# An mLSTM, mixture-of-experts and ELU network on one core: recurrent state by float16 products and DMA copies, with a new order of the pieces

## The chip, the core and the metric

The kernel runs on one core of one Trainium2 chip. The core has TensorE (matrix products, results in PSUM), VectorE, ScalarE, GpSimd (POOL in the profile) and SyncE (SP), which here only starts transfers, and 16 DMA engines. The metric is the device time of one execution in microseconds (us).

## The reference

```
attention, per (b, h) and token t, D = 40, 2 x 8 heads, 768 tokens:
  m' = max(f + m, i); fs = exp(f + m - m'); is = exp(i - m')
  C = fs C + is v k^T;  n = fs n + is k
  y = sigmoid(o) * (C q) / max(|n q|, 1)
x = rows of y, 1536 x 320
experts: logits + log1p(exp(x w_noise)) * noise, best two of 8 per row, softmax weights
  x = sum over both of weight * (relu(x w1[e]) w2[e]),  w1 320 x 1024, w2 1024 x 320
last layer: out = ELU(x w_in) w_out,  w_in 320 x 2048, w_out 2048 x 320
```

Inputs and output are float32 (the last layer's weights reach the kernel as float64 words, from which it makes float32 itself).

## The kernel before, in words

The 1536 tokens are 12 chunks of 128, six for each batch, and chunks 0 to 5 are also the first half of the rows, 6 to 11 the second. The first piece of work is the gates (lines 498 to 528): the gates come in as 16 rows of 768, a scan on VectorE makes the running maximum, TensorE turns them into columns (`gate_cols`, L508), and two products with constant masks (L521, L522) and exponentials give the decays of every chunk.

Then, for each chunk (`attention`), k and q are split into float16 parts of 40 rows each, three parts to a head, turned on TensorE (L704, L705) and multiplied (L707); the product is masked (L709 or L710 with L712). The state of a batch (`st`, 40 x 8 x 41, float32) is carried from chunk to chunk: TensorE adds the new outer products (L676) to the old state, which a float32 product with the unit matrix puts into the same PSUM sum (L681), and VectorE multiplies by the decay (L684). For the heads of the next chunk the state has to be in 120 rows: high part, low part and high part again. That is made by a float32 product with a threefold unit matrix (`rep`, L686), a copy on ScalarE that rounds it to float16 (L690), and a VectorE piece that takes the high part away in the middle 40 rows (L691). The heads (L742, L745) then give the chunk's output, which is divided, multiplied by the sigmoid and handed to `token_rows`.

`token_rows` finds the greatest value of each row (L631 or L632), makes a power of two of it and its inverse (L634, L636), splits the row into float16 parts (`split_row`), stores it in DRAM (`x_rows`), turns it on TensorE (`turn_row`, L589) and multiplies it with the router's weights (L646); L649 scales the logits. After the last chunk of a half, `router` picks two experts for each row and makes the lists of rows for each expert.

There are 16 jobs, expert by half (`expert`). A job gathers its rows by indirect DMA (L977), has them turned by DMA (L585, on SP's queue), multiplies them with the expert's first weights (`contract`, L941, in four pairs of hidden blocks) and with its second weights (L954, L955, L957). All float32 weights are split into two float16 parts on ScalarE and VectorE when they arrive (L386, L397). After all jobs the rows are gathered again, mixed, and go through the last layer.

None of this is issued in the order of the code. Each call of `do` (class `Order`) records a piece with its inputs, outputs and the engines that may run it. `run` decodes the table `ORDER`: each number is four times the index of a piece, in the order in which the code records them, plus the choice of its engine. So the table fixes for every engine in which order it issues its work, DMA starts included, and an engine that waits for one piece holds up all that stands behind it:

```
order = np.frombuffer(zlib.decompress(base64.b85decode("".join(table.split()))), "<u2").tolist()
order = [divmod(x, 4) for x in order]
for i, j in order:
    ...
    op["ways"][j][2]()
```

Of the kernel before, what the change touches and what calls it, by code (L numbers as in the profile page):

```python
# [71 lines left out]
c-jTQZRC1;f&lREIp=$xpP!$;=hUTL4J{2VT^f4P($LVZhL(n2bm`L4i)J-6G_?HwH1wjSOG`sbLzk9bbZN+HX=!O_XlPbLFS;}|v~+3M&j$bq3LuWvF$N  # L72
TY02E*V2OtmyF^~WatO81)3J?|tH4w$#SO&DP6i9<4Xkrl01AsR{8yjFbFvU99uQ3K6VqGxD1iS^hSOb*70$XAuJdTgBf5RLsgV%wAPw^f$!FynX8~6~PU
|BqgId~R~@eizzbwD4iu)o1eL<URZDSVCX@EktF5kAMS_yDv)9-n|Mo5s^vj!>{IzQ;G%7BjE|Ucd`Po><^TT)=i%6fY8E5W`FOxA+||<G;gC_yaE!P2!1
Ph&^^DD#Q{`U={p~zwn<DJ)%uq@Hf7~KM_}=ir4U;69=qHtnnKGh$Gg5kmwU#;)D%|Hv9lz;x&SSbI^q&Fa%RjCq#(gkYI=gJ|aGYcjA9Bfl!DJykHF?iz
zS$Ki~pfu^je<W8#-^LNxIMJ0%SGARHKn29d|^*o=4*|BS!k1|;ABj$sE+LYL^l8F;}yxdd(eS8xjo7$T++kVEp%*o$}*b0SLo2hqcy7$S!-1tFP+Gx*oU
8Y~F_A)LbuWXLm{AU@$)7$-*Xg{_Fs$RiNQ4>AW2AW5dk8@48X2=`z>Zix-CfJ>Mn`uGa2;RbGDj9P&%{yDKHVq^gh@Hlw|OEOJn$OM@se@lEr{x=+vMYx
9wxg#^g0VatOJi;CEKV*_B!wSriHTWgW5@&dV7m%Qi#ECeNSC}Uo&>(MY3`=2a@&=pm4jnQ|Jz$+_Fmb9tRjDtiBDNv_o;s3aaz{0p7Sm=rOqb~~A55PaF
hgd<jF}U823xW~PM9-Ur~ZjrQ!DC1PMHarqKf2<nUX7}M3$&Eb0wS9g}s9fwPCi@jGU7@b_cdhn!1rYrcCXbEA^tv<O5V;h00LhQdz1*KS7Qv(s$|&{!Ep
ypO80tLEgz0bzrV+g)Y-aW>4j*Cv~9ORF&*dUFt6spikgI_oyRPBLQ}&?<}M{^obhK5Ay%WGWH94&sOO(^`seEpnLQU{40H8F3g2`kqZ4mzv&uXCqF2RG3  # L80
YY`8J2ml3e%^rOq2X2)gT>uL<>xvzA+W-O(MEMx5+X6WKHG;0Cj-_YR)W}C_SW_G^8Nbq8Z9zj%*bZI0pMUiI@@9BHQ$fKCuQjp{MkW?vg!nPAk-3(J!`!
#pwmTq@zrX5h%cosW+=|CN-hrjKfW-E;pkROoDc(C6lC+%!*DiX*xysxh$P#zNXeRqBiv3(OY^)@3;lEr1Erv%P?6c#}sJD?ddy{XOi53KGA=md)$aCFhy
p-Js5^NaAl^#q__*+<F9m@t1>l4V2|_%H{=x7U>z2*Q8vcL*#w(p5f|lBY>eA;B__>g*eo08p3IobaBn8ZzL-2a<+5CcE^tL|!WGyWTW1?=iK}o6uF00UB
# [1332 lines left out]
```

## Time and profile before

| | |
|---|---|
| time, median of three runs | 468.0 us (467.3 to 468.56) |
| the profiled execution | 472.35 us, span 470.6 us |
| TensorE busy | 440.8 us, 94% of the span |
| VectorE busy | 380.8 us, 81% |
| ScalarE busy | 300.8 us, 64% |
| GpSimd busy | 94.4 us, 20% |
| mean granted clock of TensorE | 0.984 |

The span runs from the first to the last instruction. A matmul's record is longer than the distance to the next one, since matmuls overlap; where work stands back to back, the pieces of the chain of waits show the pace. Float32 products have two records each.

### The profile page before, as it was taken

How to read it: one execution, taken by the hardware profiler on the slowest of the kernel's cores; microseconds unless marked ns; L12 is line 12 of the kernel's file. 1: busy time of each engine (PE TensorE's matmuls, PEld its weight loads, DVE VectorE, ACT ScalarE, POOL GpSimd, SP SyncE). 2: the span in 40 equal slices, each digit the busy share in tenths (PEclk: the TensorE clock that was granted, in tenths of full speed). 3: DMA queues.
4: the chain of work that ended last, by engine and by line, in shares of the span. 5: the costliest groups of instructions: out<-in, count | busy, mean ns of one | idle time of the engine just before them, and what ended most of it. 6: DMA issues, size and time to landing. Idle time of an engine off the chain costs nothing.

```text
span 470.6 us, 10573 instructions
## 1 busy us (share of the span) xinstructions
PE 440.8 (94%) x4094; PEld 372.1 (79%) x4094; DVE 380.8 (81%) x853; ACT 300.8 (64%) x519; POOL 94.4 (20%) x110
## 2 busy tenths in 40 slices
PE   4999889788899999999989999899999999999994
PEld 4788877677788979888868888788888877887873
DVE  5889999988998987998787897498788949678780
ACT  4798998675766764565564345398785765667640
POOL 3223125513121012112203102521321120000000
PEclk9999999879999999999989999999999999999999
DMA  9979574799996799799787942433302320001001
GB/s 132 175 138 183 143 138 102 204 238 245 241 302 185 217 239 299 188 198 262 207 231 223 262 142 63 114 91 33 72 21 79 84 43 30 1 27 31 1 31 33
DMA packets 102554, 66.43 MB, mean 141 GB/s; under 512 B 79216, under 2 KB 94112, under 8 KB 102496
## 3 DMA queue, kind: packets, MB, share of 16 engines
q1 hardware_dynamic: 99616, 57.27, 51.3%
q0 software_dynamic: 2816, 8.31, 6.8%
q8 instruction: 34, 0.56, 0.5%
q14 instruction: 24, 0.20, 0.1%
q10 hardware_dynamic: 64, 0.10, 0.1%
HBM read 50.87 MB, written 8.52 MB: 126 GB/s over the span
## 4 chain that ended last, share of the span: by engine, by line
PE 65%; DMA 14%; DVE 11%; ACT 4%; issue 3%; SPq 1%; POOL 1%; ACTq 0%; DVEq 0%
PE S L941 28%; PE O L954 10%; PE O L955 10%; PE O L957 9%; DMA sw<-in_moe_w 5%; DMA sf<-in_moe_w_in 3%; DVE wa L397 2%; PE O L742 2%; PE S L676 1%; DVE wb L397 1%; DMA xT<-xg 1%; DMA kt<-in_k 1%; PE T L704 1%; DMA x_rows<-xr 1%; DVE xr L397 1%
## 5 line engine op out<-in xcount | busy, mean ns | idle before, releaser
L941 PE MATMUL S<-xT,wa 128*128 128x224 f16 (+1 forms) x1024 | 102.0, 259 | 5.2 <-DMA xT<-xg 3.0
L941 PEld LDWEIGHTS <-wa 128*128 128x128 f16 x1024 | 95.2, 100 | 9.0 <-DMA xT<-xg 2.6
L941 PE MATMUL S<-x3T,fwa 128*128 128x256 f16 x768 | 88.7, 273 | 1.2 <-DMA x3T<-x3r 1.2
L941 PEld LDWEIGHTS <-fwa 128*128 128x128 f16 x768 | 75.1, 98 | 11.7 <-issue 1.5
L954 PE MATMUL O<-wb,hidden 128*128 128x320 f16 (+1 forms) x256 | 75.6, 300 | 2.1 <-ACT yo L377 0.9
L955 PE MATMUL O<-wb,hidden 128*128 128x320 f16 (+1 forms) x256 | 75.5, 300 | 0.0
L957 PE MATMUL O<-wb,hidden 128*128 128x320 f16 (+1 forms) x200 | 60.0, 300 | 0.7 <-DVE hidden L998 0.7
L977 POOL DMA_INDIRECT xg<-x_rows,table x32 | 36.0, 1126 | 114.7 <-DMA xT<-xg 94.0
L954 PE MATMUL O<-fwb,gh 128*128 128x320 f16 x192 | 57.4, 299 | 0.0
L955 PE MATMUL O<-fwb,gh 128*128 128x320 f16 x192 | 57.4, 299 | 0.0
L996 ACT ACTIVATE hidden<-S 128x448 f16<-128x448 f32 (+1 forms) x64 | 32.4, 512 | 25.3 <-PE S L941 25.0
L1159 DVE SCALAR_TENSOR_TENSOR ex<-ex,th 128x512 f32<-128x512 f32 x48 | 33.4, 697 | 14.1 <-ACT ex L1157 7.2
L998 DVE SCALAR_TENSOR_TENSOR hidden<-S,hidden 128x128 f16<-128x128 f32 (+2 forms) x92 | 39.8, 455 | 4.9 <-ACT hidden L996 4.6
L1158 ACT ACTIVATE re<-S,sca 128x512 f32<-128x512 f32 x48 | 32.9, 691 | 13.4 <-DVE gl__5588 L397 4.5
L1156 ACT ACTIVATE th<-S,sca 128x512 f32<-128x512 f32 x48 | 33.0, 686 | 13.1 <-PE S L941 13.0
L1157 ACT ACTIVATE ex<-S,sca 128x512 f32<-128x512 f32 x48 | 32.8, 686 | 10.3 <-PE S L941 9.5
L1119 POOL DMA_INDIRECT yg<-y_rows,rows_i x24 | 25.0, 1043 | 66.2 <-DVE fwb L397 27.9
L1160 DVE SCALAR_TENSOR_TENSOR re<-ex,re 128x512 f32<-128x512 f32 x48 | 32.9, 689 | 3.7 <-ACT re L1158 1.7
L1075 ACT ACTIVATE nm<-sf 128x320 f32<-128x320 f32 (+1 forms) x28 | 16.1, 576 | 28.5 <-DVE fwb L397 8.8
L955 PEld LDWEIGHTS <-hidden 128*128 128x128 f16 (+1 forms) x256 | 26.9, 105 | 8.9 <-issue 2.0
L954 PEld LDWEIGHTS <-hidden 128*128 128x128 f16 (+1 forms) x256 | 26.9, 105 | 7.9 <-ACT hidden L996 0.9
L397 DVE SCALAR_TENSOR_TENSOR wa<-sw,wa 128x1024 f16<-128x1024 f32 x24 | 28.9, 1217 | 4.0 <-ACT wa L386 3.8
(251 smaller groups left out, 864.5 us busy)
## 6 DMA issues: line engine op xcount, KB each, us to landing
sw<-in_moe_w SPq DMA_DIRECT2D x16, 512.0 KB, 4.3
sw<-in_moe_w SPq DMA_DIRECT2D x16, 480.0 KB, 4.3
sf<-in_moe_w_out SPq DMA_DIRECT2D x16, 320.0 KB, 3.7
sw<-in_moe_w SPq DMA_DIRECT2D x16, 256.0 KB, 5.1
sf<-in_moe_w_in SPq DMA_DIRECT2D x8, 512.0 KB, 5.8
sw<-in_moe_w SPq DMA_DIRECT2D x8, 320.0 KB, 4.5
y_rows<-yo SPq DMA_DIRECT2D x16, 160.0 KB, 4.4
sf<-in_moe_w_in SPq DMA_DIRECT2D x8, 256.0 KB, 4.9
```

The lines of the kernel that those rows point to most:

```text
L397: some(on, [("V", 0.07 + 0.06 * m + 1.04e-3 * n, lambda: V.scalar_tensor_tensor(dst(), src(), scale(), hi(), op0=OP.mult, op1=OP.subtract) ...
L941: PE.matmul(acc, wa[:, r, w, f * P:(f + 1) * P], xT[:, j, :n], start=(i == 0), stop=(i == 7))
L954: PE.matmul(o, a, wb[:, 0, f % FB], start=(f == 0), stop=False)
L955: PE.matmul(o, a, wb[:, 1, f % FB], start=False, stop=(not b and f == last))
L957: PE.matmul(o, b[0], wb[:, 0, f % FB], start=False, stop=(f == last))
L977: do([("G", 1.1, lambda: G.indirect_dma_start(out=xg()[:n], out_offset=None, in_=(x_all if hf else x_rows[0]())[:, :], in_offset=bass.Indi ...
L998: vec(2 * n, lambda x=x, n0=n0, n=n: V.scalar_tensor_tensor(hi(x, n), src(n0, n), 0.0, hi(n0, n), op0=OP.max, op1=OP.subtract), [ph, hid[f ...
L1156: act(512, lambda: A.activation(th(), pf(), AF.Tanh, scale=sca()[:, 2:3]), [pf, sca], [th], "exp", 1)
L1157: act(512, lambda: A.activation(ex(), pf(), AF.Exp, scale=sca()[:, 1:2]), [pf, sca], [ex], "exp", 1)
L1158: act(512, lambda: A.activation(re(), pf(), AF.Relu, scale=sca()[:, 1:2]), [pf, sca], [re], m=1)
L1159: vec(512, lambda: V.scalar_tensor_tensor(ex(), ex(), 1.0, th(), op0=OP.add, op1=OP.mult), [ex, th], [ex], port=True)
L1160: vec(512, lambda: V.scalar_tensor_tensor(re(), ex(), 0.0, re(), op0=OP.min, op1=OP.add), [ex, re], [re], port=True)
```

## The change

What it does, part by part:

- **Constant products.** Eight pieces of three products of 384 columns each, of constants, into columns of a PSUM bank that nothing reads.
- **State.** L681 becomes two float16 products with the unit matrix, of the state's high part and its low part. L686, L690 and L691 go. Instead a high part (40 rows, ScalarE or VectorE) and a low part (VectorE) are made from the state in SBUF, and two DMA copies per step bring the high part to rows 80 to 119 and the low part to rows 40 to 79 (20 copies in all). The high and low parts have three buffers.
- **First jobs.** The rows of jobs (0, 0), (1, 0) and (2, 0), six tiles, are turned by five transposes each on TensorE and one copy from PSUM, instead of by DMA.
- **Row scales.** The power of two of a row is made for six chunks at once, and the logits of a half are scaled in one piece; per chunk one small VectorE piece is left and a plain copy of the logits on VectorE or ScalarE. The scratch of the row maximum on ScalarE is the row buffer itself.
- **Constants.** `rep` and `less` and the clearing of the state go.
- **Order.** A new table, of 2025 pieces against 2009. Decoded, it has one piece of constant products ahead of the gate turns, one before L521, one after L522 and five between pieces of the attention (chunks 2 to 11). All 20 copies stand on SP. Nine of the ten high parts are on ScalarE, and nine of the twelve logit copies. The first expert products stand behind the logits of chunk 11, where they stood behind those of chunk 9. Ahead of the second half's L813 stand three pairs of hidden blocks (four before) and seven VectorE splits of expert weights (nine before). In SP's order the second weight load of expert 0 stands behind the row store of chunk 5 and the third behind the loads of k, q and v of chunk 11; before, both stood among loads of chunks 6 to 8. Further on the order differs in many places.

The diff, with the lines of the table left out:

```
--- before.py
+++ after.py
@@ -42,13 +42,15 @@
 NBLK = 256
 
 WIDE = 120
+FILL = 8
+EARLY = ((0, 0), (1, 0), (2, 0))
 
 SQ, SK, SV = 16.0, 4.0, 64.0
 SO = SQ * SK * SV
 SW = 128.0
 SIN, SOUT = 64.0, 128.0
 
-ON = dict(k3="A", q3="AV", vw="V", s3h="GA", s3l="V", ph="A", pl="GV", vh="VA", vl="V", y="G", xr="AVG", turn="AV",
+ON = dict(k3="A", q3="AV", vw="V", s3h="AV", s3l="V", ph="A", pl="GV", vh="VA", vl="V", y="G", xr="AVG", turn="AV",
           kq="AV", yo="VA", wh="AV", hv="VA", wl="V", q3l="V")
 PREC = "112111111111"
 
@@ -69,42 +71,42 @@
 
 
 ORDER = """
...
 """
 
 PASSES = ((0, 0, 0), (0, 1, 0), (1, 0, 1), (1, 1, 1), (3, 0, 0), (4, 0, 1), (2, 0, 2), (2, 1, 2))
@@ -507,6 +509,9 @@
         for c in range(NCH):
             PE.transpose(quarters(p())[:, j, c * BH:(c + 1) * BH], x()[:, o + c * P:o + (c + 1) * P], id32()[:BH, :BH])
 
+    for _ in range(FILL):
+        te(3, 384, lambda: [PE.matmul(bank[:, :384], ones16(), ones16()[:, None].to_broadcast([P, 3, P]),
+                                      start=True, stop=True) for _ in range(3)])
     vec(1, lambda: V.memset(mt()[:, 0:1], -1e30), [], [mt])
     vec(2 * S, lambda: V.tensor_tensor_scan(mt()[:, 1:], gf(), gi(), -1e30, op0=OP.add, op1=OP.max), [gf, gi], [mt])
     te(12, P, lambda: [gate_cols(p1, gf, 0, 0), gate_cols(p1, gi, 0, 1)], [gf, gi], [p1], rows=BH, busy=BH)
@@ -569,7 +574,7 @@
         pool(128, lambda: G.affine_select(out=before(), in_=before(), pattern=[[1, P]], compare_op=OP.is_gt,
                                           fill=0.0, base=0, channel_multiplier=-1), [before], [before])
 
-    inv2 = fixed([P, NT], F32, "inv2")
+    inv2, top = fixed([P, NT], F32, "inv2"), fixed([P, NT], F32, "top")
     logits = fixed([P, NT, 2 * E], F32, "logits")
 
     def split_row(xr, x, scale, r):
@@ -587,21 +592,12 @@
             return
         pt = ps_t()
         te(5, P, lambda: [PE.transpose(pt()[:, x, :n], xr()[:n, x * P:(x + 1) * P], id16()[:n, :n])
-                          for x in range(5)], r, [pt], w)
+                          for x in range(5)], r, [pt], [x[0] if isinstance(x, tuple) else x for x in w])
         copy(5 * n, lambda: dst()[:, :, n0:n0 + n], lambda: pt()[:, :5, :n], [pt], w, 0.52e-3, ON["turn"])
 
 
     st = [fixed([P, H, D1], F32, f"st{b}") for b in range(B)]
-    rep = fixed([P, 3, D], F32, "rep")
-    V.tensor_copy(rep(), id32()[:, :D].unsqueeze(1).to_broadcast([P, 3, D]))
-    for x in st:
-        V.memset(x(), 0.0)
-    less = fixed([P, 1], F32, "less")
-    G.memset(less(), -1.0)
-    for lo_row, step in ((-D, 1), (2 * D - 1, -1)):
-        G.affine_select(out=less(), in_=less(), pattern=[[0, 1]], compare_op=OP.is_ge, fill=0.0, base=lo_row,
-                        channel_multiplier=step)
-    s3 = {}
+    s3, slo = {}, {}
     U = {}
 
     def chunk(x, t):
@@ -625,17 +621,13 @@
 
         b, c = divmod(t, NCH)
 
-        am, sc = a_([P, 1], F32, "am"), a_([P, 1], I32, "sc")
-
-        far = a_([P, DM + 1], F32, "far", 1)
+        sc, xr = a_([P, 1], I32, "sc"), a_([P, ROW], F16, "xr", 3)
+        am = lambda: top()[:, t:t + 1]
         do([("V", 0.07 + 1.04e-3 * DM, lambda: V.tensor_reduce(am(), y(), axis=AX.X, op=OP.max, apply_absolute_value=True)),
-            ("A", 0.22 + 0.83e-3 * DM, lambda: A.activation(far(), y(), AF.Abs, scale=1.0 / 64, accum_out=am()))],
-           [y], [am])
-        chain([(1, lambda: V.tensor_scalar(inv2()[:, t:t + 1].bitcast(I32), am().bitcast(I32), EXPM, None,
-                                           op0=OP.bitwise_and)),
-               (1, lambda: V.tensor_scalar(sc(), inv2()[:, t:t + 1].bitcast(I32), EXPM, None, op0=OP.bitwise_xor))],
-              [am], [inv2[t], sc])
-        xr = a_([P, ROW], F16, "xr", 3)
+            ("A", 0.22 + 0.83e-3 * DM, lambda: A.activation(xr()[:, :DM + 1], y(), AF.Abs, scale=1.0 / 64, accum_out=am()))],
+           [y], [top[t], xr])
+        vec(1, lambda: V.tensor_scalar(sc(), am().bitcast(I32), EXPM, EXPM, op0=OP.bitwise_and, op1=OP.bitwise_xor),
+            [top[t]], [sc])
         split_row(xr, lambda: y()[:, :DM], lambda: sc().bitcast(F32), [y, sc])
         load(lambda: [(x_rows[b]()[c * P:(c + 1) * P], xr())], [x_rows[b]], [xr])
         xT, lg = a_([P, 5, P], F16, "xTt"), ps_l()
@@ -646,8 +638,7 @@
                 PE.matmul(lg()[:, :2 * E], xT()[:, j], (rwl if w else rwh)()[:, r], start=(n == 0), stop=(n == 7))
 
         te(8, 2 * E, logit, [xT, rwh, rwl], [lg])
-        vec(80, lambda: V.tensor_scalar(logits()[:, t], lg()[:, :2 * E], inv2()[:, t:t + 1], 0.5 / SW,
-                                        op0=OP.mult, op1=OP.mult), [lg, inv2[t]], [logits[b]])
+        copy(2 * E, lambda: logits()[:, t], lambda: lg()[:, :2 * E], [lg], [logits[b]])
 
     def attention(t):
         b, c = divmod(t, NCH)
@@ -669,7 +660,7 @@
 
 
         if c < NCH - 1:
-            pc, pr = ps_s(), ps_s()
+            pc = ps_s()
 
             def add():
                 for h in range(H):
@@ -677,19 +668,21 @@
                               stop=(not c and h == H - 1))
 
             te(H, 4 * D1, add, [kt, vw_], [pc])
+            flat_ = lambda x: x().rearrange("p h d -> p (h d)")
             if c:
-                te(1, 4 * n1, lambda: PE.matmul(pc()[:D, :n1], id32()[:, :D], st[b]().rearrange("p h d -> p (h d)"),
-                                                start=False, stop=True), [st[b], pc], [pc])
+                te(2, n1, lambda: [PE.matmul(pc()[:D, :n1], id16()[:D, :D], flat_(x)[:D], start=False, stop=i == 1)
+                                   for i, x in enumerate((s3[t], slo[t]))], [s3[t]["hi"], slo[t], pc], [pc])
             eb = lambda: egl()[:D, row(t + 1)].unsqueeze(2).to_broadcast([D, H, D1])
             vec(n1, lambda: V.tensor_tensor(st[b]()[:D], heads_of(pc()[:D]), eb(), op=OP.mult), [pc, egl], [st[b]])
-            s_ = s3[t + 1] = a_([SD, H, D1], F16, "s3")
-            te(1, 4 * n1, lambda: PE.matmul(pr()[:SD, :n1], rep().rearrange("p j d -> p (j d)"),
-                                            st[b]().rearrange("p h d -> p (h d)"), start=True, stop=True),
-               [st[b]], [pr], [s_])
-            full = lambda: heads_of(pr()[:SD])
-            act(n1, lambda: A.activation(s_(), full(), AF.Copy), [pr], [s_])
-            vec(n1, lambda: V.scalar_tensor_tensor(s_(), s_(), less()[:SD], full(), op0=OP.mult, op1=OP.add),
-                [pr, s_], [s_])
+            s_, lo = s3[t + 1], slo[t + 1] = a_([SD, H, D1], F16, "s3", 3), a_([D, H, D1], F16, "slo", 3)
+            sb = lambda: st[b]()[:D]
+            high(n1, lambda: s_()[:D], sb, lambda: 1.0, [st[b]], [s_["hi"]], on=ON["s3h"])
+            low(n1, lo, sb, None, lambda: s_()[:D], [st[b], s_["hi"]], [lo], on="V")
+            for o, key, src in ((2 * D, "top", lambda: s_()[:D]), (D, "mid", lo)):
+                def copied(e, o=o, src=src):
+                    e.dma_start(s_()[o:o + D], src())
+                do([("G", 0.75, lambda f=copied: f(G)), ("SP", 0.4, lambda f=copied: f(SP))],
+                   [s_["hi"] if o > D else lo], [s_[key]], late=1.4, dma=0.12)
 
 
         kq = []
@@ -787,6 +780,10 @@
         nl, eq, sel = tl("nl", HT, E), tl("eq", HT, E), tl("sel", HT, E, dt=F16)
         best, pick, r = tl("best", 2, HT), tl("pick", 2, HT, E), tl("r", HT)
 
+        vec(HT, lambda: V.tensor_scalar(inv2()[:, ts].bitcast(I32), top()[:, ts].bitcast(I32), EXPM, None,
+                                        op0=OP.bitwise_and), [top[t] for t in range(hf * HT, hf * HT + HT)], [inv2[hf]])
+        vec(100, lambda: V.scalar_tensor_tensor(logits()[:, ts], logits()[:, ts], 0.5 / SW, bc(inv2()[:, ts], 2 * E),
+                                                op0=OP.mult, op1=OP.mult), [logits[hf], inv2[hf]], [logits[hf]], port=True)
         act(50, lambda: A.activation(nl, logits()[:, ts, E:], AF.Sigmoid, scale=-1.0), [logits[hf]], [me], "sigmoid")
         act(50, lambda: A.activation(nl, nl, AF.Ln), [me], [me], "ln")
 
@@ -978,7 +975,7 @@
                     out=xg()[:n], out_offset=None, in_=(x_all if hf else x_rows[0]())[:, :],
                     in_offset=bass.IndirectOffsetOnAxis(ap=table[hf]()[:n, e, i:i + 1], axis=0)))],
                    [table[hf], *x_rows[:hf + 1]], [xg], late=1.7, dma=0.75 * n / P)
-                turn_row(xg, n, xT, n0, [xg], [xT[n0]])
+                turn_row(xg, n, xT, n0, [xg], [xT[n0]], (e, hf) in EARLY)
             tile_(n0, n, i, m_([P, ROW], F16, "xg", 4))
         do.due = due
         wa, wb = W[e]
```

## Rows read from the trace of the kernel before

**Rows 1.** The page, busy us (share of the span) and instructions of each engine.

```profile
PE 440.8 (94%) x4094; PEld 372.1 (79%) x4094; DVE 380.8 (81%) x853; ACT 300.8 (64%) x519; POOL 94.4 (20%) x110
```

**Rows 2.** Stretches: busy us (instructions) by engine, granted clock, DMA share, GB/s.

```profile
10.00:40.00 30.00, 29.02 (x344) 24.55 (x345) 26.07 (x79) 24.42 (x42) 8.22 (x12) 1.00 0.88 162
70.00:80.00 10.00, 9.50 (x128) 7.75 (x126) 9.96 (x29) 8.82 (x17) 4.99 (x4) 1.00 0.46 112
90.00:100.00 10.00, 8.38 (x90) 7.55 (x91) 8.64 (x26) 7.10 (x12) 4.74 (x5) 0.52 0.98 240
104.00:302.00 198.00, 188.54 (x1692) 162.86 (x1690) 166.34 (x343) 111.30 (x199) 39.83 (x36) 0.99 0.84 218
```

**Rows 3.** The chain of waits from 0 to 20 us: start, length, what.

```profile
6.19 1.47 PE O L508 x12
10.41 0.33 PE T L704
14.76 0.11 PE T L704
15.50 0.06 PE T L704
```

**Rows 4.** The chain again, its state products, and a load.

```profile
16.58 0.74 PE S L686 x2
17.32 0.68 PE S L681 x2
31.83 0.60 PE S L686 x2
37.93 0.68 PE S L681 x2
50.50 4.82 DMA kt<-in_k
```

**Rows 5.** The chain where it runs along VectorE (first of many such pieces).

```profile
67.26 1.21 DVE wa L397
```

**Rows 6.** Groups by line on VectorE: busy us, mean ns of one, idle before.

```profile
L691 DVE SCALAR_TENSOR_TENSOR s<-s,less,S 120x328 f16<-120x328 f16 x10 | 5.4, 543 | 0.0
L649 DVE TENSOR_SCALAR logits<-bank,inv 128x16 f32<-128x16 f32 x12 | 2.8, 230 | 0.4 <-PE bank L646 0.2
L634 DVE TENSOR_SCALAR inv<-am 128x1 int32<-128x1 int32 x12 | 1.7, 142 | 0.2
```

**Rows 7.** Timelines of VectorE (L684, the state) and TensorE (L742, heads).

```profile
40.90 0.48 DVE L684 TENSOR_TENSOR st<-S,egl 40x328 f32<-40x328 f32 x1
44.92 0.43 PE L742 MATMUL O<-vw,pw 128*128 128x120 f32 x2
...
61.39 0.49 DVE L684 TENSOR_TENSOR st<-S,egl 40x328 f32<-40x328 f32 x1 [0.51 <-PE S L681]
67.13 0.43 PE L742 MATMUL O<-vw,pw 128*128 128x120 f32 x2
...
79.98 0.48 DVE L684 TENSOR_TENSOR st<-S,egl 40x328 f32<-40x328 f32 x1
84.53 0.32 PE L742 MATMUL O<-vw,pw 128*128 128x120 f32 x1
```

**Rows 8.** DMA issues: KB each and median us from issue to landing.

```profile
x_rows<-xr SPq DMA_DIRECT2D x12, 160.0 KB, 3.9
out<-zo SPq DMA_DIRECT2D x12, 160.0 KB, 1.8
```

**Rows 9.** The chain, sixteen products of 192 columns at either level of the clock.

```profile
92.22 2.57 PE S L941 x16
196.27 1.32 PE S L941 x16
```

**Rows 10.** The timeline of TensorE, second half's first slot product.

```profile
103.49 0.18 PE L813 MATMUL bank<-sel,before 128*128 128x48 f16 x1 [0.43 <-DVE sel L806]
```

**Rows 11.** TensorE's waits from 86 to 140 us: total, times, longest.

```profile
PE S L941 <- DMA xT<-xg: 1.4, 2, 0.8
```

More of the change, by code (lines that the diff above doesn't have):

```diff
@@ L71 @@
 ORDER = """
[L72 to L81, printed above, removed]
@@ new lines @@
+EyyfsKhha$~c^3eOQX5l2VFl*kijBtZ}uf+^%0x5*8@B4)%EPZDJm5`Yx2zYrC4PE5%p{spdLJN(x;ME;0x2uP-g0ud${Y>zL9K6XL|*p^rlcVt40up*Jh
+f53-WiO8Wxyi82Uf5Df?KM^x>N96DnnZ>K<37?aB@)rca_QV0%BEKR3nVev0>WqiU3tqsBWQ5F+4t7DtSRStsHS|Cni4$=qzQK;j8@x&!$Qkx~;);~WESV
+!O#0{wv|4x+2zms$9N8*OJh$e9(DkOr|(K}JX?|7T3k}2x9_yftH58_F5hzA}eYvdCzpa}T~f+SxEfhuT^_#?rPG4e_-$U2#$8l*^em@d;}GSrQXlUb_I4
+45G^V#dsbnKCnG&Irh_$P@XVyps>IMzyIY@+2?hN92+`Pzz?ste7>kVOHdk`VZ<;>Wb&7E(MS+BcOG9O<t%YbEX>TiK)>|dPANW20c*?`oe6<7l}|;hM>N
+n8Wcens3ujU7z&^^4e2}kBA#rE5~#nCEZropRG$jdC8|sb^o<ImE%bYGKt<@!Nr*;Jg;MD|#V}2@P2QLm-KOu%gHo6W^E;|TJ}H73QZMGobjcUnCTw&>b?
@@ new lines @@
+7b~r2##n$JCrQD4Tjq#pnt3XBtv}q6rRR1*S(LT$~P52|7XnrbqYbDK#LMw9QQDDLtbJHc2ZS!+u46N&8HU`H=aR3NsNTMX%^NwWj;zh-{;28l@x5f)dyV
+yP{&$pU4E0WKzt}RFsLLU(p}aQHtR<be4wPj!AG)F3qI5Exn`n^q$Gl2YN{f+>!o}>Yy1W%jB3mQ(#W?nNCm}D#;}&z@@k_m!}K#n);5)a2NUw^9fgCcGR
+3J(ce>LMq#h?jegL-r7LuWsWNpY!o}DIbEgl?fqim6(QoM(_o7jzNH>|!nK)Nt;%tIVvNpHk2tLK8*$kUyb8Mb1utj#kmDnX$W-Dxo%W-+`#g#dfuW(hi$
+`!aZ2iO`{=eFE|Tk$p4X6r1&Z}|qh<BD8^YjJ0;#~!&R*Jn4}fW2{hZpgN|2H)d4+=v~sCvL)aIg!6`Q})V@xI4Gz<9vdDa0_<M&e*^5JHE-c`97!cEgtY
+ae#v(D72D;L{E)Z#6u)Q3-1q#1hkTfy^G#L}`+S;@@B==|$M_MS;ivqVKk!+e5WeJ+!h$aeGoBHa{MX!(PYJe|=hMQJ%kgFY!V5x$Zwm!JBb@j%|KN}8mC
@@ new lines @@
+p(}AukjJASwbBhg@B(3Nx-Kl!b{<5#I1Mp)NFpt<V&1e2KsFO|d7m*rXU1fzTJ;@-@CC41_h?5uSWkc=3o35o{qNMumqs6z0N6fb2p@iDO|YOof?{7FR+<
+Y=}3ZB}T=ya1b^^R@@0k;Uwh5I=>eS(q1?V8@4IM#JK1S3GpdhgqL_?U&2**ig#fxO~jt~OCc`w#fN~1Q?bnsL_(a2Eh#TDVpuqdZLuQ?Vn;fNXYnE)#jD
+sA%hF9mq>a>-%Hme)OLws-m861L6cchqs)$1oN^ixev=(DhNvuk3sV9x3urv}Q(pVfwHE}1^q`EYf=Hf;iOAC>ZQu0umNHZxeHKc_!ml)}tBuE2!C7q?Qe
+32&dRT|1SNs)kLO9^2rkK}jaOukEq{GGUzH}YIw$O-8oo#glOR^G`O>C7gjm3)=c@>;&gH~B7SB|=Wh5BVuSB}92ijJ%gS>_I-5zm^19Q1;S6ddVx1P^xl
+Cww0lBlp~6w9Ho;~lNlu^#gvS!$YHrI1EnlOWu#1$l@e7d@>rQFK#s_HIj$s>nUa-r@?6;}e^z$lQdui$X{T(Ij1pD~@>$s{2gQ+(N>L`%s2o)r@`bIdHz
@@ new lines @@
+lcLm6MWFE=o$dD-R_vrInbRS8{4o-K$rnpfu%*vSpvj&kCY8R7EW+KxI@xwN<E=l#ZNGKTsp;=Q5O&YD%ptCp9j&)P_=1>WZz!)VNw!(&|+$s$KaDIirTP
+zMNG{YE$VbZMCeP)r*=}59(3<AN8(w)Sfz2*Jf9Js0Fp6LhY@JXc4Wiw&j5;XgzJDKDC<qx$;zB>R2T-M4zZ#rKil*qPEee>P+n`bFHMU)ugsj7iv`NYm7
+Efx~!@VwUJiV1{%=DT1rc62koU1`b3**ZKa~Ew6!+V7TQKD>Pu~_{Y`7>F)gd@^sau^GFn{QYYFYBU9_vVR8Lw?%WF5SpaK1^J+zWu)+_o}t?Db))}h|kz
+tC%XT_5Njy|3@ot-jY8UC?8CRU7MyKGY|mp^x;L-qgR=n_5_}X>t8it)WHqmbTQR`dn{oS9S(ET0&pxQ+=Ul^@E-S8IT1@{iv_?6gcT;od6g8s^|2So&z_
+%tCc_+<Us)x0RyU_3@Ts>1fYPl{?PAw8_dB|CyczFGcx*1FBptb19h+f2xx#MP>j#O5v;)m0MG)!5R4vxMjxEO0OXAh*n%!7n_(krtiT!AM$t$ZF=GhAY}
```

42 lines of the change are left out of this document (16 added, 26 removed).

## The prediction

> **What bounds the kernel now.** I read the page's busy line first, then the stretches of ten microseconds, then the chain of waits, and last the groups by line. TensorE is busy 94% of the 470.6 us span [rows 1]: any gain that lasts has to be TensorE time or a hole in it. The stretches [rows 2] show three stages. From 10 to 40 us TensorE is at work for 29.0 of 30 us, VectorE has 3.9 us free and ScalarE 5.6; here the chain runs along TensorE. From 67 to 92 us the chain runs along VectorE instead [rows 5], which is at 9.96 of 10 from 70 to 80 us. From 90 to 100 us the granted clock is 0.52, the lower level (1.2 GHz). From 104 to 302 us, the experts, TensorE has 9.5 us of holes in 198; after that comes the last layer, which the change does not touch.
>
> The run behind this trace took 472.35 us, the span and 1.75 us around it; the median of the runs shown is 468.0. I work out a difference on the trace and take it off the median.
>
> **Constant products among the gates.** Numbering the pieces as they are listed shows where the new order puts the eight: one ahead of the gate turns, one before the products of L521, one after L522, and five between later attention pieces. Before, neighbouring turns start 0.11 us apart until 15 us, afterwards 0.06 us [rows 3]: the clock was at its lower level, with TensorE in work without a break only from the first turn at 10.41 us. The two pieces beside L521 and L522 make the work continuous from 7.66 us, where the turns of L508 end [rows 3]. If the clock rises as much earlier, 2.75 us of work run at double rate: 1.4 us gained. Bounds: 2.5 us (all 4.9 us of turns and products from 10.41 to 15.3 at the higher level) and a loss of 1 us (the pieces themselves delay L521). I take -1.3. The five later pieces are 15 products of 384 columns, 0.16 us each at the rate of [rows 9] (sixteen of 192 columns in 1.32 us, so 0.083 us for 192): 2.5 us; one of the five stands in the stretch to 38 us (next part), and of the other four I let 0.5 fall on the path.
>
> **State by float16 products.** Ten replications (L686) and eight carries (L681) run in float32, two records each, 0.60 to 0.74 us per pair. Up to 38 us, four of each lie on the chain, 2.8 and 2.7 us (the first and the last of both fours stand in [rows 4]). The new carry is two products of 328 columns; a product of 192 columns takes 0.083 us [rows 9], so a pair takes 0.28 us and four take 1.1. Gross: 2.8 + 2.7 - 1.1 = 4.4, less 0.5 for that constant piece, 3.9. VectorE's free 3.9 us in the same stretch are just enough for all of it to count; I take -3.0, with bounds 0 (the loads, at a DMA share of 0.88 [rows 2], hold the pace) and -3.9.
>
> On VectorE each state step loses the sign correction of L691 (0.54 us) and gets a subtraction of 40 x 328 elements [rows 6], for which the product of the same size stands, 0.48 us (L684) [rows 7]. ScalarE's copy becomes the new high part on nine steps of ten. That is nearly a wash.
>
> **The DMA copies.** No row shows a copy from SBUF to SBUF, so it is bounded by the nearest rows: a store that lands in 1.8 us when nothing else is moving (`out`), and one of 3.9 us in the loaded stretch (`x_rows`) [rows 8]. The new path from the state is 0.5 (L684) + 0.5 (high) + 0.4 (low) + 0.5 (issue) + landing: 3.7 to 5.8 us, against some 2 us of the old one (0.6 for L686, a ScalarE copy, 0.5 for L691). What hides it is the distance from the state's step to the heads of the next chunk that read it. Three of the ten distances are short: 40.90 to 44.92 us, 61.39 to 67.13 and 79.98 to 84.53, that is 4.0, 5.7 and 4.6 us [rows 7]; the other seven are wider. At 3.7 us nothing is late; at 5.8 us, 1.8 + 0.1 + 1.2 = 3.1. I take +1.0. All 20 copies stand on SP, where loads are queued behind a copy that waits for VectorE; a load in that place has its buffer's wait anyway, and I price it inside the bounds.
>
> The Trainium skill, "DMA: Bandwidth & Descriptors", section "Anatomy of one DMA — SWDGE (gpsimd) path", says a transfer costs about 2.0 us fixed plus its bytes over 436 GB/s; for 26 KB (40 x 656 bytes) that makes an estimate of 2.1 us and, by that rule, no lateness at all, and 461.0 where I come to 462.0. The loaded row of 3.9 us speaks against taking a fixed cost alone where other transfers are in the queues.
>
> **Row scales once per half.** Twelve steps on one element of VectorE (0.142 us) go, two small ones and two of 96 elements come; twelve evictions of logits (0.230 us) become copies, nine of them on ScalarE [rows 6]. Against that, VectorE takes two turned tiles of the early jobs, one more of several small copies and two more masks than before. Adding these up to the second half's slot products (L813, 103.49 us [rows 10]), VectorE has 0.7 us less to do, and two expert weight splits (1.1 us each, 2.2; one of 1.21 in rows 5) and one job's low part (0.5) come after that point instead of before: 3.4 us less ahead of it. This is the stage that VectorE bounds; I count -2.5, with bounds 0 and -3.4. ScalarE gets some 1.5 us more, mostly evictions, and has more room (8.8 of 10 in 70 to 80 us). The scratch of the row maximum now lies in the row buffer itself (three buffers), so a row store that lands late can hold ScalarE earlier; 0 to 1 us, taken as 0 because its cover is ScalarE's free time.
>
> **First jobs' rows turned on TensorE.** Six tiles: 30 transposes of 0.06 us, under 2 us of TensorE; three of the six tiles fall where TensorE has holes. In exchange TensorE no longer waits for xT by DMA in that stretch, 1.4 us in two waits [rows 11]. I take -1.0 for this with the SP and DMA time it frees, bounds +1 and -2. But the new order puts the first expert products behind the logits of the last chunk, where they stood behind those of the tenth; three pairs of hidden blocks precede L813 instead of four. One pair is 16 products of 192 columns, 1.3 us [rows 9], to be done later: +1.3, bounds 0 and 2.6. The dip of the clock from 91 to 101 us stays, since TensorE is left with transposes and logits alone for as long as before.
>
> **Sum.** -1.3 - 3.0 + 0.5 (constant pieces) + 1.0 - 2.5 - 1.0 + 1.3 = -5.0. The six other replications and four other carries fall where loads or VectorE set the pace; I count them as if two of the ten lay on the path, at 0.60 us less the 0.1 us of float16 products that they leave behind: -1.0, bounds 0 and -4. That makes -6.0. The expert stage carries this on if the weights arrive as early relative to it. Up to L813 the same weight loads have been issued in both orders, and the DMA transposes of six tiles are gone from the busiest stretch (share 0.98 from 90 to 100 us), so I leave the 6 us as they are. 472.35 - 6.0 = 466.3 for a profiled run, and 468.0 - 6.0 = 462.0 for the median.
>
> **Rivals.**
> - More is won (456): the whole VectorE term (-3.4), the rows at hand earlier, and no dip of the clock. At the lower level the first expert pair took 2.57 us, against 1.32 [rows 9]; with two such pairs and ten transposes some 3 us, and the rest from an order that closes holes among the experts. For: the 9.5 us of TensorE holes between 104 and 302 us [rows 2]. Against: the first products stand later than before. Chance 0.24.
> - It moves nothing (467): TensorE time is taken out, but loads and VectorE set the pace of attention, and what is won there is waited for again at the expert weights, since DMA is at 0.98 when the experts begin [rows 2]. For: VectorE's own load falls by only 0.7 us. Against: ten long TensorE products lie on the chain itself. Chance 0.15, two thirds of it within 0.3%.
> - Slower (470.5): the copies land behind the loads on the one SP queue. From a landing of about 4 us on, the shortest distance between state and heads is overrun; at 5.5 us (a path of 7.4) the three short distances are late by 3.4, 1.7 and 2.8, 7.9 us together, a fourth begins to be late, and TensorE, which works in order, stands in each. That makes 462.0 - 1.0 + 7.9 = 469, with the loads held up behind the waiting copies some 470.5. For: a load of `kt` sat 4.82 us on the chain at 50.5 us [rows 4]. Against: the copies are a sixth of a load's bytes. Chance 0.16.
>
> **How the numbers follow.** The forecast, 462.0, has 0.45 with its own range of 458.5 to 465.5. The range of 8 in 10 goes from 455 to 470: it takes in the no-change case and most of the slower one, and half of the richer one. About 0.3% (1.4 us) is what a measurement of this kernel can tell from no change. Faster: 0.45 + 0.24 + a third of 0.15, 0.74; within 0.3%: 0.10; slower: 0.16.
>
> **What would show it.** In the changed trace: turns 0.06 us apart from about 12.5 us on; no float32 state product, pairs of 0.28 us in its place; L813 of the second half at about 98 us instead of 103.5; heads that start without a wait for a copy; a granted clock of 0.5 for some ten microseconds around the first expert job. I am wrong if the heads wait for `s3` by DMA for more than 3 us in sum, if the gain at L813 is there but gone at 300 us, or if the second half's slot products come no earlier.

## The result and the profile after

The changed kernel took 460.9 us (median of four runs, 459.6 to 461.4), the kernel before it 467.9 (467.3 to 468.6) on the same chip: ratio 0.9845, interval 0.982 to 0.987. Timed twice more, each time beside the kernel before, it took 464.5 us (458.6 to 466.8; ratio 0.9928, 0.9901 to 0.9955) and 460.7 us (460.4 to 462.1; ratio 0.9825, 0.9789 to 0.9861). One run of the changed kernel (466.8) and one of a variant below (467.7) stood over 1.5% above the fastest of their kernel and are left out from here on, which makes 464.0 of the 464.5. The median of the 14 runs left is 461.2 us; I call it the base below. The gain is 7.0, 3.8 and 8.2 us in the three timings. The forecast was 462.0.

The busy line of the page after, which answers to [rows 1] (busy us, share of the span, instructions):

```profile
PE 436.1 (95%) x4128; PEld 369.8 (81%) x4128; DVE 382.2 (83%) x845; ACT 299.1 (65%) x525; POOL 95.9 (21%) x105
```

The stretches of [rows 2] in the kernel after (us, busy us with instructions for PE, PEld, DVE, ACT, POOL, then granted clock, DMA share, GB/s):

```profile
10.00:40.00 30.00, 29.44 (x391) 26.34 (x390) 27.51 (x79) 26.96 (x49) 8.00 (x10) 1.00 0.81 155
70.00:80.00 10.00, 8.93 (x119) 8.24 (x118) 9.93 (x27) 7.89 (x16) 3.60 (x4) 1.00 0.55 154
90.00:100.00 10.00, 9.22 (x105) 8.18 (x103) 8.86 (x33) 8.24 (x13) 0.00 (x0) 0.90 0.86 236
104.00:302.00 198.00, 191.60 (x1740) 166.86 (x1738) 170.41 (x352) 117.10 (x208) 43.37 (x40) 1.00 0.81 213
```

From 10 to 40 us more gets done in the same time: VectorE is at work for 27.51 us instead of 26.07, ScalarE for 26.96 instead of 24.42, and TensorE, at work about as long as before, gets through 391 products instead of 344. The clock between 90 and 100 us is 0.90 instead of 0.52, but the dip has only moved: from 84 to 92 us it is 0.57 (the row stands in the part on the prediction).

The two slot products, of the first half and the second, first in the kernel before, then in the kernel after (duration min/median/max, first and last start):

```profile
L813 PE MATMUL bank<-sel,before x2: 183/190/197, 61.9 to 103.5; 128*128 128x48 f16 x2
...
L810 PE MATMUL bank<-sel,before x2: 182/182/182, 57.1 to 95.8; 128*128 128x48 f16 x2
```

The first comes 4.8 us earlier, the second 7.7 us. The stretch up to the second one, in the kernel before and in the kernel after:

```profile
10.00:103.49 93.49, 85.31 (x1022) 73.71 (x1023) 84.98 (x269) 76.44 (x132) 29.30 (x32) 0.95 0.77 161
...
10.00:95.80 85.80, 78.47 (x1025) 69.66 (x1024) 80.27 (x243) 75.40 (x141) 28.33 (x29) 0.96 0.82 175
```

TensorE's busy time falls by 6.8 us and its idle time by 0.9, from 8.2 to 7.3. So most of the 7.7 us is TensorE work that no longer stands ahead of this point. In the further profiles of the same two kernels, described below, the busy time is 83.24 us before and 77.76 and 79.76 us after.

The first product of the last layer came at 302.4 us before and comes at 291.1 after, 11.3 us earlier; from there both need 170.0 us. The timed gain is 7.0 us, not 11.3: the profiled execution of the kernel before is 4.4 us above its median, that of the kernel after within 0.3 us of its own.

### The profile page after: what moved, and what is told of

Its sections match the earlier page's. It is cut to its first block, busy times and chain, and to the rows that moved or that the text cites. A ratio compares the mean times of both kernels' runs of the same rounds, so it can differ in the third digit from the quotient of the medians.

```text
span 459.3 us, 10628 instructions
## 1 busy us (share of the span) xinstructions
PE 436.1 (95%) x4128; PEld 369.8 (81%) x4128; DVE 382.2 (83%) x845; ACT 299.1 (65%) x525; POOL 95.9 (21%) x105
## 4 chain that ended last, share of the span: by engine, by line
PE 57%; DVE 17%; DMA 12%; ACT 7%; issue 4%; SPq 1%; POOL 0%; ACTq 0%; DVEq 0%
PE S L938 24%; PE O L951 8%; PE O L952 8%; PE O L954 8%; DMA sw<-in_moe_w 5%; PE O L735 4%; DVE hidden L995 2%; DVE wa L399 2%; DVE wb L399 2%; DMA sf<-in_moe_w_in 2%; DMA yg<-y_rows,rows_i 1%; DMA sf<-in_moe_w_out 1%; DMA xT<-xg 1%; DVE nm L383 1%; DVE na L1078 1%
## 5 line engine op out<-in xcount | busy, mean ns | idle before, releaser
L938 PE MATMUL S<-xT,wa 128*128 128x224 f16 (+1 forms) x1024 | 99.4, 256 | 1.1 <-DMA xT<-xg 0.8
L938 PEld LDWEIGHTS <-wa 128*128 128x128 f16 x1024 | 93.7, 99 | 4.2 <-DVE na L1078 1.0
L938 PE MATMUL S<-x3T,fwa 128*128 128x256 f16 x768 | 88.3, 273 | 2.9 <-DMA x3T<-x3r 2.9
L1154 ACT ACTIVATE ex<-S,sca 128x512 f32<-128x512 f32 x48 | 32.4, 685 | 11.2 <-PE S L938 11.2
L1116 POOL DMA_INDIRECT yg<-y_rows,rows_i x24 | 26.3, 1098 | 49.6 <-DVE x L1122 23.1
L1157 DVE SCALAR_TENSOR_TENSOR re<-ex,re 128x512 f32<-128x512 f32 x48 | 34.2, 712 | 2.9 <-ACT re L1155 0.8
```

The lines of the kernel that those rows point to most:

```text
L938: PE.matmul(acc, wa[:, r, w, f * P:(f + 1) * P], xT[:, j, :n], start=(i == 0), stop=(i == 7))
L1154: act(512, lambda: A.activation(ex(), pf(), AF.Exp, scale=sca()[:, 1:2]), [pf, sca], [ex], "exp", 1)
L1157: vec(512, lambda: V.scalar_tensor_tensor(re(), ex(), 0.0, re(), op0=OP.min, op1=OP.add), [ex, re], [re], port=True)
```

## The experiments

**The old pieces in the new order.** The kernel before, its pieces issued in the sequence of the new table; where the new one has a copy, a constant piece or a step once per half, nothing stands.

```diff
 ORDER = """
-(table of the kernel before)
+(its pieces at the places that they have in the new table)
```

> The pieces of before in the new order (replication and its two copies stand where the high and low parts stand, the early rows are turned by DMA from the place of their TensorE turns, no constant pieces). Theory P: no gain, 466 to 471 us, since the float32 products are back on the path. Rival O: 460 to 463 us.

478.0 us (474.1 to 480.1), ratio 1.0195 (1.0143 to 1.0246): slower than before by 10 us. The order by itself is no gain. ScalarE's waits there from 10 to 100 us (us in total, times, longest), first row:

```profile
ACT s L689 <- PE S L685: 13.9, 7, 3.3
```

ScalarE, which works in order, stands 13.9 us in front of the replication that TensorE has yet to reach. In the kernel before the same wait is 1.8 us in five times. The stretch up to the second slot product, which comes at 112.9 us in this kernel:

```profile
10.00:112.90 102.90, 87.35 (x1007) 73.84 (x1008) 83.69 (x258) 73.83 (x131) 25.45 (x29) 0.92 0.68 144
```

TensorE is idle for 15.6 us of it, against 8.2 in the kernel before: the holes are most of what the order costs the old pieces.

**The new pieces in the old order.** The changed kernel; each new piece stands where its forerunner stood: high part and its copy behind the state's step, low part and its copy where the sign correction was.

```diff
 ORDER = """
-(table of the changed kernel)
+(its pieces at the places that their forerunners have in the table before)
```

> All pieces of the change, issued in the order of before (a new piece takes the place of the one it replaces; stores of rows 0, 1, 2 and 5 and the turned tiles are moved as far as their buffers need). Theory P, the gain is TensorE time taken out of the path (float32 state products, early clock) and the order only fits it: 462 to 465 us, L813 of the second half at about 98 to 100 us. Rival O, the gain is the new order: 467 us or more, L813 at 103 or later.

508.6 us (506.6 to 510.5), ratio 1.0879 (1.0831 to 1.0928). SP's waits at the copies from 10 to 100 us, the five longest of eleven groups:

```profile
SPq L683 <- ACT s L388: 10.0, 2, 6.7
SPq L683 <- DVE sc L629: 6.2, 2, 5.5
SPq L683 <- ACT q L388: 5.1, 1, 5.1
...
SPq L683 <- DVE slo L403: 4.2, 2, 2.5
SPq L683 <- ACT xr L627: 4.0, 2, 3.4
```

The copies wait at the head of SP's queue for 40.4 us in sum, with loads behind them (15.4 us in the changed kernel); TensorE is at work for 22.87 of the 30 us to 40. The mechanism of the slower rival is seen here: copies that wait for other engines hold SP's queue. How much of the 47 us the queue accounts for is not shown, since other pieces were moved too.

**The new front, the old rest.** The changed kernel in the new order up to the second half's slot products, then in the old one.

```diff
 ORDER = """
 (table of the changed kernel up to the second L810)
-(the rest of that table)
+(the remaining pieces in the sequence of the table before)
```

> The changed kernel, its order kept up to the second half's slot products and the order of before from there on. If the gain is made ahead of the experts and only carried on (my prediction): within 1.5 us of the changed kernel, 460 to 462.5 us. Rival, the order among the experts gives part of it: 464 to 466 us, with more TensorE holes between the slot products and the last layer.

468.1 us (464.8 to 471.2), ratio 1.0003 (0.997 to 1.0036). The slot products come at 96.3 us, so the front is won (7.2 us), yet the last layer begins at 297.1 and the time is that of before. The stretch behind the seam, first in this kernel:

```profile
94.00:104.00 10.00, 5.39 (x62) 4.33 (x60) 7.31 (x22) 5.99 (x9) 0.00 (x0) 1.00 0.77 194
```

and in the changed kernel:

```profile
94.00:104.00 10.00, 9.22 (x102) 7.61 (x100) 9.47 (x28) 6.73 (x11) 0.00 (x0) 1.00 0.80 220
```

TensorE loses 3.8 us here, and more later: from 98 to 305 us it waits 3.0 us for xT and 2.5 for wa. From the slot products to the last layer this kernel needs 200.8 us, the changed kernel 195.3 and the kernel before 198.9. So the gain at the front is lost when the old order follows it; 1.9 us of this go beyond the old order's own time and may belong to the seam.

**The kernel before once more**, one profiled execution.

```diff
 (nothing changed)
```

> The kernel before once more, for a second profile. The trace of before has a hole and a fallen clock between 240 and 247 us, and its execution took 4.4 us longer than the median. If that hole is of that one execution, the last layer starts near 298 us here and not at 302.4; if it is of the kernel, it is here again.

472.4 us again in the profiled execution, with the slot products at 102.9 and the last layer at 302.5. One stretch of it:

```profile
210.00:250.00 40.00, 36.85 (x327) 31.98 (x325) 32.54 (x64) 23.02 (x43) 5.92 (x5) 0.96 0.85 220
```

The first profile has 37.37 us of TensorE at a clock of 0.96 there, the kernel after 39.77 at 1.00. The hole is there again, so it is not of one execution; whether the unprofiled runs, some 4 us shorter, have it too, no trace shows.

**The changed kernel twice more**, as a base.

```diff
 (nothing changed)
```

> The changed kernel again, beside the three variants of it, as their base. Both theories: 461 us (459.5 to 462.5), ratio 0.985. One thing is open: the profiled executions of the kernel before stood 4.5 us above its own median and showed the last layer 11 us later than the changed kernel; if the true difference is the timed one, 7 us, a second profile of the changed kernel should again lie within 1 us of its median.

> The changed kernel once more, as the base of the three variants beside it. In the first comparison its runs stood at 459.6 to 461.4 us, in the second at 458.6 to 466.8, while those of the kernel before stayed within 1.4 us. If the changed order has itself become sensitive, single runs scatter by 4 us or more here too; if the second comparison was disturbed by its chip, they lie within 2 us around 461.

464.0 and 460.7 us (above). In the first of the two the profiled execution was the fastest, 458.6 us, and the others reached 462.0 to 465.3 at much the same mean clock; the second stayed within 1.7 us. The kernel before did not scatter like this beside the first of them (467.2 to 468.6). What sets the scatter is open; differences under some 2 us are not told apart below.

**State in float32 again.** Replication and carry as float32 products on TensorE and no copies; all else, and the order, as changed.

```diff
-    te(2, n1, lambda: [PE.matmul(pc()[:D, :n1], id16()[:D, :D], flat_(x)[:D], ...) for i, x in enumerate((s3[t], slo[t]))], ...)
+    te(1, 4 * n1, lambda: PE.matmul(pc()[:D, :n1], id32()[:, :D], flat_(st[b]), start=False, stop=True), ...)
...
-    high(n1, lambda: s_()[:D], sb, ...)
+    PE.matmul(pr()[:SD, :n1], rep().rearrange("p j d -> p (j d)"), flat_(st[b]), start=True, stop=True)
+    A.activation(s_(), full(), AF.Copy)
-    low(n1, lo, sb, None, lambda: s_()[:D], ...)
+    vec(n1, lambda: V.scalar_tensor_tensor(s_(), s_(), less()[:SD], full(), op0=OP.mult, op1=OP.add), ...)
-    e.dma_start(s_()[o:o + D], src())
```

> The changed kernel with the state as before: replication and carry as float32 products on TensorE, no copies; the rest and the new order stay, so each replication stands where the high part stood. My theory (terms of the prediction): four replications and four carries on the path up to 38 us, 4.4 us, two more later, 1.0, less the copies' 1.0: 4 to 5 us slower, 465 to 466, with the heads of the first tiles each about 1 us later than the one before. Rival A: loads and VectorE set the pace and the float32 products cost nothing: 461 to 462. Rival B: the order is made for the copies (the replication waits for its eviction in a place where another instruction has to wait behind it): 470 or more, as with all the pieces of before in the new order (478).

473.9 us (472.2 to 476.6), ratio 1.012 (1.0099 to 1.0141): 9.9 us above the changed kernel beside it, 12.7 above the base, rival B. The slot products come at 107.9 us, 12.1 later. ScalarE's and VectorE's longest waits from 10 to 100 us in this kernel:

```profile
ACT s L693 <- PE S L691: 12.7, 7, 3.3
ACT kq L379 <- PE T L713: 2.4, 4, 1.1
...
DVE s L697 <- ACT s L693: 5.9, 5, 2.6
DVE st L685 <- PE S L682: 1.8, 4, 0.6
```

and in the changed kernel the ones at the same place:

```profile
ACT s L388 <- DVE st L676: 1.3, 2, 1.0
...
DVE st L676 <- PE S L667: 0.6, 1, 0.6
DVE st L676 <- PE S L673: 0.5, 1, 0.5
```

The wait of the old pieces in the new order is back, 12.7 us, and VectorE inherits 5.9 of it. TensorE itself waits 2.8 us for a bank that the replication's result still holds. What this is worth is read from TensorE, the busiest engine. The stretch up to the second slot product in this kernel, and the first and last state product on its chain of waits:

```profile
10.00:107.90 97.90, 86.73 (x1043) 72.93 (x1042) 82.11 (x244) 75.50 (x141) 25.18 (x29) 0.97 0.67 146
...
13.87 0.81 PE S L691 x2
...
77.08 0.76 PE S L691 x2
```

TensorE is at work for 86.73 us, against 78.47 in the changed kernel (77.76 to 79.76 in its three profiles), and idle for 11.2, against 7.3: of the 12.1 us, 8.3 are TensorE's own work and 3.8 are idle time. Of the 18 float32 pairs, 14 lie on the chain here, 9.2 us in sum; in the changed kernel three pairs of float16 products do, 1.2 us (four and five, up to 2.0 us, in its other profiles). So the larger part of what this edit saves in the new order is TensorE time, and the smaller part is idle time, with two engines that wait for TensorE's queue.

**Without the copies.** The high part is written to all 120 partitions at once, zeros beyond the first 40; the products with the low part and the second high part are left out of the result.

```diff
-            high(n1, lambda: s_()[:D], sb, ...)
+            high(n1, lambda: s_()[:SD], lambda: st[b]()[:SD], ...)
...
-                    e.dma_start(s_()[o:o + D], src())
+                    return None
```

> The changed kernel without its 20 copies: the high part is written to all 120 partitions of the state's tile at once (zeros beyond the first 40), so the products with the state's low part and the second high part are left out of the result, at the same instruction count on every engine but SP. My theory: the copies are hidden (no TensorE wait names one), worth 0 to 1 us: 460 to 461 us, or 0 to 1 below its base. Rival: their 15 us of issue on SP, and the waits of the copies at the head of that queue (12 us between 10 and 100 us), hold up the loads behind them; then without them the attention stage shortens and it is 3 us or more below its base.

461.9 us (460.0 to 465.4), ratio 0.9848 (0.9804 to 0.9893), against 460.7 beside it: nothing is won. The copies are hidden, as far as some 2 us can be told. SP's waits from 10 to 100 us in this kernel, first row, suggest why SP's time doesn't count:

```profile
SPq L369 <- DVE xr L399: 23.3, 8, 7.0
```

That wait was 9.3 us with the copies: the row stores now stand at the head of the queue, for the same split rows.

**Each copy issued twice**, to the same place.

```diff
-                    e.dma_start(s_()[o:o + D], src())
+                    return [e.dma_start(s_()[o:o + D], src()) for _ in range(2)]
```

> The changed kernel with each of the 20 copies issued twice, one straight behind the other, to the same place; this doubles their bytes, and their time on the SP queue goes from 20 to 40 issues of 0.75 us. My theory: the copies are hidden by the distance to the heads that read them, and SP has room, so at most 1 us slower, 461 to 462.5. Rival: the landing or the queue is on the path (predicted at +1.0 us, and +9 in the slower rival); then twice the issue delays heads and loads in each of ten steps, and it is 5 us or more slower, 466 or later, with heads that start without all their copies' sources being the last thing.

506.3 us (505.1 to 510.6), ratio 1.0842 (1.0809 to 1.0875). This did not test what it was made for: the second copy, to the same place, waits on SP until the first has landed, which I had not priced. SP's waits from 10 to 100 us:

```profile
SPq L683 <- DMA s<-s: 15.0, 8, 3.9
SPq L683 <- DMA s<-slo: 12.5, 7, 2.5
```

It gives the landing time that the trace after lacks: 27.5 us in 15 waits, 1.8 us each behind the issue, 3.9 at the longest. These waits and 20 further issues, some 42 us in all, are not hidden; whether 20 issues more without such waits would be hidden wasn't tried.

**Without the constant products.**

```diff
-                                      start=True, stop=True) for _ in range(3)])
+                                      start=True, stop=True) for _ in range(0)])
```

> The changed kernel without its eight pieces of constant products, nothing else touched. My theory: the three early pieces raise the clock some 1.3 us earlier (0.7 us of time), the five later ones cost 0.5 us and give nothing, so without them it is 0 to 1 us slower, 461 to 462, and the turns at 12 us stand 0.11 us apart until about 15 us. Rival A: the later pieces fill TensorE's gaps and hold the clock through attention; without them the granted clock between 40 and 130 us falls below 0.9 and it is 3 us or more slower, 464 or later. Rival B: the pieces cost their own time, eight times 0.5 us; without them it is 2 us or more faster, 459 or less.

460.4 us (460.0 to 462.2), ratio 0.9845 (0.9827 to 0.9863): 3.6 us below the changed kernel beside it, 0.8 below the base, and level with that kernel's other two timings (460.9 and 460.7). No loss is shown; a small gain is not excluded. TensorE's timeline in this kernel (start, length, line, operation, out<-in, tile):

```profile
10.00 0.33 PE L697 MATMUL T<-id,k 128*120 128x128 f16 x1 [0.30 <-DVE k L399]
...
11.86 1.32 PE L667 MATMUL S<-vw,kt 128*40 128x41 f32 x16
13.11 1.03 PE L700 MATMUL S<-kq 120*128 120x128 f16 x8
...
14.15 0.25 PE L697 MATMUL T<-id,k 128*120 128x128 f16 x1
14.23 0.22 PE L698 MATMUL T<-id,q 128*120 128x128 f16 x1
14.29 0.22 PE L697 MATMUL T<-id,k 128*120 128x128 f16 x1
...
15.05 0.81 PE L667 MATMUL S<-vw,kt 128*40 128x41 f32 x16
```

and in the changed kernel:

```profile
12.38 1.26 PE L667 MATMUL S<-vw,kt 128*40 128x41 f32 x16
13.57 0.62 PE L700 MATMUL S<-kq 120*128 120x128 f16 x8
14.03 0.22 PE L697 MATMUL T<-id,k 128*120 128x128 f16 x1
14.09 0.22 PE L698 MATMUL T<-id,q 128*120 128x128 f16 x1
...
15.01 0.81 PE L667 MATMUL S<-vw,kt 128*40 128x41 f32 x16
```

The turns (L697, L698) start 0.11 us apart at first and 0.06 us apart later. Without the constants the pace doubles at about 14.15 us; with them it has doubled by 13.6, for the eight products of L700 take 0.62 us instead of 1.03. But without them the turns start at 10.00 instead of 10.53, since the pieces stand in front of L526 and of the turns. At the second L667 (the outer products of the second chunk) the two are level, 15.05 and 15.01.

One profile of each does not settle this, since the place where the pace doubles differs between executions of one kernel. The second profile of the changed kernel has:

```profile
10.86 0.24 PE L698 MATMUL T<-id,q 128*120 128x128 f16 x1
10.94 0.22 PE L697 MATMUL T<-id,k 128*120 128x128 f16 x1
...
14.00 0.81 PE L667 MATMUL S<-vw,kt 128*40 128x41 f32 x16
```

In its third profile the pace doubles at about 13.8 us, and in the two profiles of the kernel before at about 15.2 and 14.05. The second L667 starts between 13.99 and 15.14 us in the three profiles of the changed kernel and the four of its variants below and above that keep the constants and this stretch (the new front, no copies, row scales, early rows by DMA). So the constants may win 0 to 1 us there; the times do not show it. That the slow pace is the lower level of the clock is read from the doubled spacing alone: the granted clock in the rows from 10 to 40 us is 1.00, before and after.

**Row scales per tile.**

```diff
-        vec(1, lambda: V.tensor_scalar(sc(), am().bitcast(I32), EXPM, EXPM, ...), [top[t]], [sc])
+        vec(1, lambda: [V.tensor_scalar(inv2()[:, t:t + 1].bitcast(I32), am().bitcast(I32), EXPM, None, ...),
+                        V.tensor_scalar(sc(), am().bitcast(I32), EXPM, EXPM, ...)], [top[t]], [inv2[t], sc])
...
-        copy(2 * E, lambda: logits()[:, t], lambda: lg()[:, :2 * E], [lg], [logits[b]])
+        vec(80, lambda: V.tensor_scalar(logits()[:, t], lg()[:, :2 * E], inv2()[:, t:t + 1], 0.5 / SW, ...), ...)
```

> The changed kernel with the row scales as before: a second one-element instruction per tile, each tile's logits scaled on their way out of PSUM by VectorE (nine of these evictions go back to it from ScalarE), and none of the two instructions on 96 elements. VectorE gets 12 times 0.14 us and 9 times 0.23 us more, 3.3 us after the 0.5 that go. My theory (predicted at -2.5 us with the deferred splits): VectorE bounds the stretch from 67 to 92 us, where a third of the twelve tiles lie, so 1.0 to 2.5 us slower than its base, with the second half's slot products 1 to 2.5 us later. Rival A: 0, since the order leaves VectorE room in other places. Rival B: evictions on an engine for which the order has not been made block the queue behind them, 5 us or more slower.

462.1 us (460.6 to 465.9), ratio 0.9868 (0.9821 to 0.9916), 1.4 above the 460.7 beside it, and inconclusive: the intervals overlap. The second slot product stands at 97.1 us, where three profiles of the changed kernel have 94.9 to 97.4.

**Early rows turned by DMA**, at the places of the TensorE turns.

```diff
-        pt = ps_t()
-        te(5, P, lambda: [PE.transpose(...) for x in range(5)], ...)
+        te(1, P, lambda: SP.dma_start_transpose(dst()[:, :, n0:n0 + n], xr()[:n, :]), r, w)
```

> The changed kernel with the six early tiles of rows turned by DMA on SP, as before, issued at the place in the order where the changed kernel turns them on TensorE; 30 transposes and six evictions less. My theory (predicted at -1.0 us for the edit): 0 to 2 us slower than its base, as TensorE waits for the rows of the first expert jobs by DMA where it did not. Rival A: no difference, as TensorE has holes there in either form. Rival B: the change lives from these turns keeping TensorE at work ahead of the experts; without them the clock is at its lower level for some 4 us longer around 85 to 95 us and the first expert products come 2 us or more later, 3 us or more slower in all.

461.0 us (459.0 to 462.9), ratio 0.9826 (0.9788 to 0.9863): no difference is told apart, rival A. The stretch from 100 to 130 us in this kernel:

```profile
100.00:130.00 30.00, 24.23 (x232) 21.25 (x230) 23.22 (x46) 16.56 (x26) 5.81 (x6) 0.89 1.02 248
```

TensorE has 27.82 us there in the changed kernel, at a DMA share of 0.98. The last layer begins at 292.3 us, against 288.7 to 292.1 in the three profiles of the changed kernel, but the slot products came early here, at 94.7; from there to the last layer it is 197.6 us, against 193.8 to 195.3. So this trace shows a cost among the experts of 2 us or more. This execution took 462.6 us, 1.5 above the median, and the medians do not show the cost.

## Why the prediction was right, and by which of its steps

The total was right, 462.0 for 461 to 464, and so was the place: the attention stage, with the gain kept through the experts. The division among the edits was not, and that the total came out is in part luck: the sum has no term for the new order, which costs 10 us with the old pieces in it, and it has the state edit too small by 6 to 9 us. Left out one at a time from the changed kernel:

| step of the prediction | its term, us | measured, us |
|---|---|---|
| constant products | -1.3, and +0.5 | not told from 0 (460.4 without) |
| float16 state | -3.0 and -1.0 | -9.9 to -12.7 (copies included) |
| copies | +1.0 | not told from 0 (461.9 without) |
| row scales, deferred splits | -2.5 | -1.4 for the scales, not told from 0 |
| early turns | -1.0 | not told from 0 (461.0 without) |
| new order | no term | +10 with the old pieces (478.0) |

- Constants: "if the clock rises as much earlier, 2.75 us of work run at double rate" takes the place of the rise from one trace, while the kernel before has it at about 15.2 us in one profile and at 14.05 in the other. The changed kernel has it at 10.9, by 13.6 and at about 13.8 us in three executions, so the forecast of "about 12.5" is neither met nor refuted, and a single trace cannot price this term. What the runs leave is 0 to 1 us at the second L667, with turns that start 0.53 us later.
- State: the step was mis-sized. I put eight of the 18 float32 pairs on the path up to 38 us and counted the other ten "as if two of the ten lay on the path", -4.0 in all. With the old path back in the new order, 14 pairs lie on the chain (9.2 us), and TensorE works 8.3 us longer up to the slot products. What I left out is smaller, 3.8 us more of TensorE's idle time: the new path from the state to the heads' operand has no TensorE in it, so ScalarE and VectorE no longer wait for its queue. With the old path ScalarE's wait is 12.7 us, in the kernel before, ordered for it, 1.8. The pair of 0.28 us was right as TensorE's pace, for its two products start 0.15 us apart at 15.75 us; on the chain, where the second product has to end, a pair takes 0.38 and 0.47 us (at 15.82 and 63.39).
- Copies: no lateness is seen. An issue takes 0.75 us on SP, for which I had 0.5, and a landing 1.8 us more, within my bounds. No TensorE wait from 10 to 98 us names a copy. The estimate made from the Trainium skill, "DMA: Bandwidth & Descriptors", section "Anatomy of one DMA — SWDGE (gpsimd) path", no lateness at all, agrees with this, though that section is about the GpSimd path and these copies are issued on SP.
- Later first products: three pairs of products do precede the slot products, as I had it; what that costs was not measured apart. The dip "for some ten microseconds" came from one trace. It lasts about 7 us here, about 7 and 3.5 in the changed kernel's other two profiles, and 10 and 7 in the two of the kernel before. The first product comes at 88.3 us (92.1 before). The stretch in the kernel after:

```profile
84.00:92.00 8.00, 6.85 (x63) 5.53 (x63) 6.93 (x22) 6.38 (x16) 4.69 (x4) 0.57 0.71 215
```

- Slot products: forecast at about 98 us, found at 95.8 (94.9 to 97.4).
- "I leave the 6 us as they are" through the experts: it held in the times, but not of itself. With the old expert order all of it is lost (468.1). In the traces the new order also shortens the way from the slot products to the last layer, 193.8 to 195.3 us in three profiles, against 198.9 and 199.6 in two of the kernel before.

My form of the sum, edit by edit on the trace of before, could not see what a new order does to the pieces that stay. By the runs, order and edits belong together: the new order alone is 10 us slower, the edits in the old order 41 us slower (508.6), both together 4 to 8 us faster. In the new order the state edit accounts for 10 to 13 of the 17 us between old pieces and new; the rest I cannot divide, since the others count for little one at a time. What the state edit would be worth in an order made for the other edits alone wasn't tried.
